# Reordering the first batch of a fused channel attention: k ahead of q, an early k norms row, zero matmuls, and folds split around the sums

## The chip, the cores and the metric

The kernel runs on one core of one Trainium2 chip. The metric is the device time of one execution in microseconds; the "span" of a profile, from the first to the last instruction, is some two microseconds shorter. Engines: PE is TensorE (matmul), PEld its weight loads, DVE is VectorE, ACT is ScalarE, POOL is GpSimd, which here starts the loads. PE is called cold while its granted clock is 0.50 (half clock). The tail is the stretch from the landing of the last piece of q and k to the first product of the main loop.

## The reference, cut to what matters

```python
def _attn_ref(q, k, v, tau):                 # q, k, v: 4 x 5824 x 256, float32
    qn = q / (np.linalg.norm(q, axis=1, keepdims=True) + 1e-06)
    kn = k / (np.linalg.norm(k, axis=1, keepdims=True) + 1e-06)
    s = kn.transpose(0, 2, 1) @ qn / tau     # 256 x 256 per batch
    a = np.exp(s - s.max(-1, keepdims=True))
    a /= a.sum(-1, keepdims=True) + 1e-09
    return v @ a
# then, on x = the result as 23296 x 256 (w1, w2: 256 x 1024; w3: 1024 x 1024; w_out: 1024 x 256):
#   ((x @ w1) * (x @ w2)) @ w3 @ w_out
```

The attention is over channels: its 256 x 256 matrix needs all 5824 rows of q and k of a batch, which are loaded in six pieces each. The kernel multiplies that matrix into w1 and w2 once per batch (the **folds**, result Wf) and w3 into w_out once (W_sb). The products of a fold land in a PSUM buffer (`psum.tile` in the code); its **drain** is the instruction on ACT or DVE that scales them and copies them to Wf. A main loop of 4 batches x 12 chunks x 8 blocks then does, per block, two products of v with Wf (a and b), the cast of a on ACT, a times b on DVE, and the product with W_sb (o).

## The kernel before: the parts concerned

The first batch has its scores made before the main loop. Squares of q and k are taken as products whose diagonal is the sum of squares.

```python
def pe_transpose(dst, src, tag, on_act):
    m = psum.tile([P, 8, P], BF16, tag=tag, ...)
    for i, blk in enumerate(src):
        nc.tensor.transpose(m[:, i, :], blk, ident_b)
    if on_act: nc.scalar.copy(dst, m)
    else:      nc.vector.tensor_copy(dst, m)
# ... first_scores(pi): for each 128-row slot of a piece, products q.k, q.q and k.k; norms_first: their diagonals
def rnorm(src):                     # 4 columns: q norms and k norms together
    r = work.tile([P, 4], F32, tag="r", ...)
    nc.scalar.activation(out=r, in_=src, func=AF.Ln)
    nc.scalar.activation(out=r, in_=r, func=AF.Exp, scale=0.5)
    nc.vector.tensor_scalar_add(r, r, 1e-6)
    nc.vector.reciprocal(r, r)
def row():                          # spreads the k norms along a row, after rnorm
    m = psum.tile([P, 512], F32, tag="ab", ...)
    for ct in range(CT):
        nc.tensor.matmul(m[:, ct * P : (ct + 1) * P],
            lhsT=st["r"][:, CT + ct : CT + ct + 1].to_broadcast([P, P]), rhs=ident, ...)
    nc.scalar.copy(kr, m[:, :C])
# ... scaled: s = G * kr (DVE), e = exp(r * s) (ACT); sums: column sums of e by 4 matmuls, reciprocal rs (DVE)
def fold(i):                        # 8 per batch
    m = psum.tile([P, 512], F32, tag="ab", ..., bufs=4)
    for c2 in range(CT):
        nc.tensor.matmul(m, lhsT=st["e"][:, c2, ...], rhs=w12[:, c2, ...], ...)
    if i % 2 == 0: nc.scalar.activation(out=dst, in_=m, func=AF.Copy, scale=st["rs"][...])
    else:          nc.vector.tensor_scalar_mul(dst, m, st["rs"][...])
# ... start of the program
for pi in range(NP_):               # 6 pieces; loads run in the order q0 k0 q1 k1 ...
    ...
    first_scores(pi)
soft0[0][1]()                                   # norms
transpose_half_on_pe(0, 0, 0, True)             # first half of v piece 0, copy on ACT
for _, fn in soft0[1:3]: fn()                   # row, scaled
transpose_half_on_pe(0, 0, 1, False)            # second half, copy on DVE
for _, fn in soft0[3:8]: fn()                   # sums, folds 0-3
```

For the later batches the same units are placed between blocks of the main loop. Each has a planned time and a planned cost; a virtual clock, advanced by these costs and by the blocks, decides behind which block a unit comes.

```python
units: norms (0.0), ss (1.0), row (0.6), scaled (0.0), sums (0.2), 8 folds (0.43 each)   # planned costs, us
ts = [t1 + 1.0, t1 + 4.0, t1 + 6.5, t1 + 8.5, t1 + 12.0] + [t1 + 13.0 + 0.9 * i for i in range(8)]
```

## Time and profile before

| | before |
|---|---|
| time, median of 3 | 585.7 us (585.57 to 585.95) |
| span | 583.6 us |
| PE busy | 564.0 us |
| first exponential (e) starts | 39.92 us |
| first a of the main loop starts | 44.35 us |

The changes of the clock are whole multiples of 3.41 us apart, so the profile was cut into stretches of that length (columns: stretch, its length, PE, PEld, DVE, ACT, POOL busy with counts, granted clock, DMA share, GB/s):

```profile
14.90:18.31 3.41, 2.63 (x36) 2.39 (x35) 0.00 (x0) 0.00 (x0) 0.78 (x3) 1.00 1.06 211
21.72:25.13 3.41, 1.45 (x20) 1.26 (x19) 0.00 (x0) 0.00 (x0) 1.06 (x2) 1.00 1.08 217
...
35.37:38.78 3.41, 1.46 (x19) 1.27 (x17) 1.73 (x4) 1.31 (x3) 1.44 (x2) 1.00 1.24 204
38.78:42.20 3.42, 2.60 (x17) 1.42 (x16) 1.68 (x5) 1.44 (x4) 0.00 (x0) 0.50 1.10 214
```

PE is busy for 1.45 of the 3.41 us before the clock falls at 25.1 us (42%). At 38.78, after a stretch with 1.46 us (43%), it falls again and stays at half over the folds. The timeline of before shows start us, duration us, engine, line, operation, out<-in, count, and in brackets the idle time of the engine and what ended it.

```profile
42.89 0.75 DVE L304 TENSOR_SCALAR Wf<-fold,rs 128x512 bf16<-128x512 f32 x1 [1.37 <-PE fold L296]
43.74 0.69 ACT L302 ACTIVATE Wf<-fold,rs 128x512 bf16<-128x512 f32 x1 [1.02 <-PE fold L296]
```

### The profile page before, as it was taken

How to read it: one execution, taken by the hardware profiler on the slowest of the kernel's cores; microseconds unless marked ns; L12 is line 12 of the kernel's file. 1: busy time of each engine (PE TensorE's matmuls, PEld its weight loads, DVE VectorE, ACT ScalarE, POOL GpSimd, SP SyncE). 2: the span in 40 equal slices, each digit the busy share in tenths (PEclk: the TensorE clock that was granted, in tenths of full speed). 3: DMA queues.
4: the chain of work that ended last, by engine and by line, in shares of the span. 5: the costliest groups of instructions: out<-in, count | busy, mean ns of one | idle time of the engine just before them, and what ended most of it. 6: DMA issues, size and time to landing. Idle time of an engine off the chain costs nothing.

```text
span 583.6 us, 10198 instructions
## 1 busy us (share of the span) xinstructions
PE 564.0 (97%) x3840; PEld 364.2 (62%) x3840; DVE 372.7 (64%) x552; ACT 339.0 (58%) x617; POOL 68.5 (12%) x145
## 2 busy tenths in 40 slices
PE   3789999999999999999999999999999999999996
PEld 3764576766666666666665766666665766566555
DVE  0026644788876567778866657777876556555564
ACT  0026635677756576767756567777766545454454
POOL 3330111221100112002100112002100000000000
PEclk9889999999999999999999999999999999999999
DMA  8999879864654699754672498764564335401011
GB/s 166 212 208 185 127 143 208 166 138 123 138 108 73 141 202 177 158 109 90 141 145 73 111 197 180 144 147 95 123 136 103 78 82 138 93 38 73 37 69 54
DMA packets 65393, 74.85 MB, mean 128 GB/s; under 512 B 45760, under 2 KB 49344, under 8 KB 65344
## 3 DMA queue, kind: packets, MB, share of 16 engines
q0 software_dynamic: 14656, 39.46, 39.1%
q1 hardware_dynamic: 50688, 34.74, 21.5%
q8 instruction: 30, 0.49, 0.3%
q14 instruction: 19, 0.16, 0.1%
HBM read 78.91 MB, written 23.86 MB: 176 GB/s over the span
## 4 chain that ended last, share of the span: by engine, by line
PE 93%; DMA 3%; DVE 1%; ACT 1%; POOL 1%; issue 1%; ACTq 0%; POOLq 0%
PE o L376 28%; PE a L354 27%; PE b L354 26%; PE G L177 5%; DMA k<-in_k_dram 3%; PE fold L296 3%; PE w L449 1%; PE G L207 1%; DVE abs L362 1%; ACT as L360 1%; PE sq L215 0%; PE sq L211 0%; PE ss L240 0%; PE row L259 0%; POOL q L106 0%
## 5 line engine op out<-in xcount | busy, mean ns | idle before, releaser
L362 DVE TENSOR_TENSOR abs<-as,b 128x512 bf16<-128x512 bf16 (+1 forms) x384 | 252.3, 658 | 158.9 <-ACT as L360 144.9
L360 ACT CAST as<-a 128x512 bf16<-128x512 f32 (+1 forms) x384 | 215.7, 562 | 174.1 <-DVE abs L362 85.3
L376 PE MATMUL o<-W_sb,abs 128*128 128x256 bf16 x1472 | 221.4, 273 | 0.2 <-DVE abs L362 0.2
L354 PE MATMUL a<-vT,Wf 128*128 128x512 bf16 x704 | 209.8, 380 | 0.1
L354 PE MATMUL b<-vT,Wf 128*128 128x512 bf16 x704 | 209.5, 379 | 0.0
L354 PEld LDWEIGHTS <-Wf 128*128 128x128 bf16 x1536 | 148.8, 98 | 97.1 <-issue 1.4
L376 PEld LDWEIGHTS <-abs 128*128 128x128 bf16 x1472 | 143.4, 98 | 86.5 <-DVE abs L362 0.4
L186 DVE TENSOR_TENSOR acc<-acc,sq 128x1024 f32<-128x1024 f32 x66 | 80.4, 1218 | 0.4 <-ACT sq L174 0.4
L346 POOL COPY gate_t<-abs 1x1 bf16<-1x1 bf16 x39 | 15.5, 398 | 396.3 <-DVE abs L362 379.6
L177 PE MATMUL G<-k,q 128*128 128x256 bf16 x276 | 50.0, 273 | 0.0
L174 ACT ACTIVATE sq<-q 128x512 f32<-128x512 bf16 x66 | 41.8, 633 | 0.0
L174 ACT ACTIVATE sq<-k 128x512 f32<-128x512 bf16 x66 | 41.6, 631 | 0.0
L207 PE MATMUL G<-k,q 128*128 128x256 bf16 x92 | 23.3, 295 | 12.0 <-DMA k<-in_k_dram 12.0
L390 DVE COPY osb<-o 128x512 f32<-128x512 f32 x44 | 30.1, 685 | 0.4 <-PE o L376 0.4
L177 PEld LDWEIGHTS <-q 128*128 128x128 bf16 x276 | 27.0, 98 | 3.1
L389 ACT COPY osb<-o 128x512 f32<-128x512 f32 x44 | 25.8, 585 | 4.0 <-PE o L376 1.9
L248 ACT ACTIVATE r<-ss 128x4 f32<-128x4 f32 x4 | 0.7, 181 | 38.5 <-DVE ss L227 35.3
L211 PE MATMUL sq<-q 128*128 128x128 bf16 x92 | 21.5, 233 | 0.0
L215 PE MATMUL sq<-k 128*128 128x128 bf16 x92 | 21.5, 233 | 0.0
L225 DVE TENSOR_TENSOR dg<-sq,ident 128x512 f32<-128x512 f32 x1 | 0.7, 691 | 31.6 <-PE sq L215 31.6
L296 PE MATMUL fold<-w,e 128*128 128x512 bf16 x64 | 17.5, 410 | 0.0
L302 ACT ACTIVATE Wf<-fold,rs 128x512 bf16<-128x512 f32 x16 | 11.0, 687 | 9.5 <-PE fold L296 9.4
(78 smaller groups left out, 199.7 us busy)
## 6 DMA issues: line engine op xcount, KB each, us to landing
out_dram<-osb SPq DMA_DIRECT2D x44, 512.0 KB, 2.8
q<-in_q_dram POOLq DMA_DIRECT2D x20, 512.0 KB, 6.1
k<-in_k_dram POOLq DMA_DIRECT2D x20, 512.0 KB, 9.0
v<-in_v_dram POOLq DMA_DIRECT2D x19, 512.0 KB, 5.2
w_bf<-in_moe_w_dram POOLq DMA_DIRECT2D x2, 1024.0 KB, 16.8
q<-in_q_dram POOLq DMA_DIRECT2D x4, 320.0 KB, 4.9
k<-in_k_dram POOLq DMA_DIRECT2D x4, 320.0 KB, 6.4
v<-in_v_dram POOLq DMA_DIRECT2D x4, 320.0 KB, 6.5
```

Of the source, the lines that this page charges most:

```text
L174: nc.scalar.activation(out=dst[:, :, part, :], in_=src[:, o : o + 2, :], func=AF.Square)
L177: nc.tensor.matmul(G[:, ct, :], lhsT=qt[:, i, ct * P : (ct + 1) * P], rhs=kt[:, i, :], start=(pr == 0 and part == 0 and ct == 0), stop=(pr ...
L186: nc.vector.tensor_add(accs[n], accs[n], sqs[0])
L207: nc.tensor.matmul(G[:, ct, :], lhsT=qt[:, i, cs], rhs=kt[:, i, :], start=(first and ct == 0), stop=(last and ct == CT - 1), skip_group_ch ...
L211: nc.tensor.matmul(S[:, ct, :], lhsT=qt[:, i, cs], rhs=qt[:, i, cs], start=(first and ct == 0), stop=False, skip_group_check=True,)
L296: nc.tensor.matmul(m, lhsT=st["e"][:, c2, c1 * P : (c1 + 1) * P], rhs=w12[:, c2, w, h * 512 : (h + 1) * 512], start=(c2 == 0), stop=(c2 == ...
L354: nc.tensor.matmul(t[:, :n], lhsT=Wf[b][:, ct, w, j * P : (j + 1) * P], rhs=rhs_of(b, c, ct), start=(ct == 0), stop=(ct == CT - 1),)
L360: nc.scalar.copy(a_sb[:, :n], tiles[0][:, :n])
L362: nc.vector.tensor_mul(ab[:, :n], a_sb[:, :n], tiles[1][:, :n])
L376: nc.tensor.matmul(tl[s // 2][:, s % 2, :], lhsT=ab[:, off : off + P], rhs=W_sb[:, j, :], start=(j == 0 and s % 2 == 0), stop=(j == FT - 1 ...
L389: nc.scalar.copy(o[:, 0:2, :], tl[0])
L390: nc.vector.tensor_copy(o[:, 2:4, :], tl[1])
```

## The change

Its intent is to have less to do after the last piece of q and k has landed. k pieces are loaded ahead of q, all held; the k norms are spread into a row by one matmul with a matrix of ones and four activations, before q is complete, so only the q norms stay in the tail. Zero matmuls keep PE's clock up. The first half of each of folds 0 and 1 runs between the two halves of the column sums. The half transpose of v, which had stood ahead of row and sums, moves behind fold 2, with its copy split between ACT and DVE; the other half moves into the main loop. The later batches use the new k row as well, with new planned costs and times. Cut below: new places for some buffers, and w1 and w2 now loaded ahead of the second half of the first v piece.

```diff
+IN_BUFS = {"q": 5, "k": 6, "v": 3}
+        if on_act is None:                                   # pe_transpose
+            nc.scalar.copy(dst[:, :4, :], m[:, :4, :])
+            nc.vector.tensor_copy(dst[:, 4:, :], m[:, 4:, :])
+    def busy(k):
+        m = psum.tile([P, 512], F32, tag="ab", ...)
+        for _ in range(k):
+            nc.tensor.matmul(m, lhsT=warm[:, :P], rhs=warm, start=True, stop=True, ...)
+        def k_row():
+            m = psum.tile([P, 512], F32, tag="ab", ...)
+            nc.tensor.matmul(m[:, :C], lhsT=ones_pp, rhs=st["ksq"], start=True, stop=True)
+            nc.scalar.activation(out=kr, in_=m[:, :C], func=AF.Ln)
+            nc.scalar.activation(out=kr, in_=kr, func=AF.Exp, scale=0.5)
+            nc.scalar.activation(out=kr, in_=kr, func=AF.Ln, bias=eps_t)
+            nc.scalar.activation(out=kr, in_=kr, func=AF.Exp, scale=-1.0)
-        head = [(0.0, norms_first)] if n == 0 else [(0.0, norms), (1.0, ss)]
-            head + [(0.6, row), (0.0, scaled), (0.2, sums)]
+        head = [(0.0, norms), (0.5, k_row), (0.4, q_sums)]
+        return head + [(0.0, scaled), (0.2, sums)] + [(0.43, lambda i=i: fold(i)) for i in range(8)]
+        def first_folds():
+            sum_mm(0)
+            fold_mm(0, 0)
+            fold_mm(1, 0)
+            sum_mm(1)
+            fold_mm(0, 1)
+            fold_mm(1, 1)
+            fold(2)
+            transpose_half_on_pe(0, 0, 0, None)
+            fold(3)
 # ... start of the program, from the first q piece; cut: the loads and squares of k0 and k1, with 22 zero matmuls
+    for pi in range(3):
+        products(pi, whole)
+        squares("q", pi, whole)
+        squares("k", pi + 2, whole)
+        busy(4)
 # ... cut: loads of q4 k5 q5, w1/w2, v
+    products(3, whole); squares("q", 3, whole)
+    products(4, whole); squares("q", 4, whole)
+    squares("k", 5, range(LAST + 1), end=True)
+    soft0[0](); busy(2); soft0[1]()              # diagonal of k, k row
+    squares("q", 5, first)
+    products(5, first)
+    squares("q", 5, rest, end=True)
+    soft0[2]()                                   # diagonal and norms of q
+    products(5, rest, end=True)
+    soft0[3]()                                   # s, e
+    busy(6)
+    soft0[4]()                                   # first_folds
 # ... in the main loop
+            at(4.0, 0.5, lambda: transpose_half_on_pe(0, 0, 1, False))
-        ts = [t1 + 1.0, t1 + 4.0, t1 + 6.5, t1 + 8.5, t1 + 12.0] + [t1 + 13.0 + 0.9 * i for i in range(8)]
+        ts = [t1 + 1.0, t1 + 3.5, t1 + 4.0, t1 + 8.0, t1 + 12.0] + [t1 + 13.0 + 0.9 * i for i in range(8)]
```

## The prediction

> **What bounds the kernel now.** I read the engine summary first, then the slices, then what TensorE (PE) waited for.
>
> ```profile
> PE 564.0 (97%) x3840; PEld 364.2 (62%) x3840; DVE 372.7 (64%) x552; ACT 339.0 (58%) x617; POOL 68.5 (12%) x145
> ...
> PE   3789999999999999999999999999999999999996
> ...
> PEclk9889999999999999999999999999999999999999
> DMA  8999879864654699754672498764564335401011
> ```
>
> PE is busy 564.0 of 583.6 us, so at most 19.6 us of idle can be removed; whatever it does cold (half clock) comes on top. The slices (14.6 us each) put the loss into the first three, before the main loop, and a little into the last. The waits of PE over the whole run say the same:
>
> ```profile
> PE G L207 <- DMA k<-in_k_dram: 12.0, 3, 8.9
> PE row L259 <- DVE r L251: 1.9, 1, 1.9
> PE sum L281 <- ACT e L274: 0.8, 2, 0.6
> ```
>
> Three waits for k pieces are 12.0 us, then 2.7 us in the softmax. No wait of size lies in the later batches. But the DMA itself is full in this stretch, as the five-microsecond windows show (columns: PE, PEld, DVE, ACT, POOL, granted clock, DMA share, GB/s):
>
> ```profile
> 10.00:15.00 5.00, 4.95 (x58) 4.47 (x57) 0.00 (x0) 0.00 (x0) 0.96 (x2) 1.00 1.08 216
> 15.00:20.00 5.00, 3.85 (x53) 3.53 (x51) 0.00 (x0) 0.00 (x0) 2.37 (x7) 1.00 1.05 211
> 25.00:30.00 5.00, 5.00 (x49) 4.42 (x47) 0.00 (x0) 0.00 (x0) 1.36 (x3) 0.66 1.08 206
> 40.00:45.00 5.00, 4.30 (x14) 1.68 (x15) 2.29 (x6) 2.20 (x4) 0.00 (x0) 0.50 1.09 210
> ```
>
> So the 12.0 us are the arrival of data at about 212 GB/s (bytes written) and mostly stay. What can go is the lag behind the last arrival. First q and k pieces are usable at 6.45 and 8.85 us, then a 512 KB piece every 2.47 us; ten pieces and two of 352 KB (1.7 us each) end at about 32.6, while the last product starts at 35.48. From there the timeline shows a serial tail:
>
> ```profile
> 35.90 0.69 DVE L225 TENSOR_TENSOR dg<-sq,ident 128x512 f32<-128x512 f32 x1 [31.55 <-PE sq L215]
> ...
> 38.02 0.18 DVE L251 RECIPROCAL r<-r 128x4 f32<-128x4 f32 x1
> 38.26 0.76 PE L259 MATMUL row<-ident,r 128*128 128x128 f32 x4 [1.95 <-DVE r L251]
> ...
> 39.92 0.91 ACT L274 ACTIVATE e<-s,r 128x256 bf16<-128x256 f32 x2 [0.49 <-DVE s L271]
> ...
> 40.99 3.57 PE L296 MATMUL fold<-w,e 128*128 128x512 bf16 x8
> ...
> 44.35 1.06 PE L354 MATMUL a<-vT,Wf 128*128 128x512 bf16 x2
> ```
>
> The folds run cold: eight 512-column matmuls are issued over 3.4 us, 0.43 us each; two lines later in the same trace warm ones are 0.21 us apart. The main loop starts at **44.35**; from there PE hardly stops.
>
> **What the Trainium skill says.** "TensorE: Matmul & The Clock Gate", Part 1, says the PE clock is halved by an activity monitor with a free-running window of about 3.4 us, and that sustained activity restores it. The trace agrees: one-microsecond windows put the changes near 11.5, 25.1, 28.5, 38.8 and 45.6 us, gaps that are multiples of 3.41 us. The page asks for about an idle window; here the window 21.7 to 25.1 had a 1.96 us wait, about 42% busy, and was followed by half clock, while 14.9 to 18.3, about 78% busy, was not. I estimate the limit lies between. Part 4 of the page adds that transposes don't count as PE activity; the trace doesn't separate that. "DMA: Bandwidth & Descriptors", Bandwidth, has 425 GB/s measured for a 16 MB load by one core whose neighbour idles; the loads here read twice what they write (f32 to bf16), some 424 GB/s, which agrees, so I take 2.47 us a piece as the floor.
>
> **The change part by part.**
>
> 1. *k ahead of q.* Same bytes, same queue, one order: k0, k1, q0, k2, q1, k3, q2, k4, q3, q4, k5, q5. By the cadence above q4 is there at 29.2, k5 at 30.9, q5 at 32.6. Gain by itself: none; it frees the k norms from the tail.
>
> 2. *Zero matmuls.* 42 of 512 columns, 0.21 us each warm. Those of the piece loop (4 per pair, 0.85 us) join 2.64 us for a q piece (16 products at 0.11, 16 squares at 0.055) and 0.88 for k: 4.4 of the 4.94 us that a pair takes to arrive, so they hide and keep the clock up. Before, half clock from 25.1 to 28.5 cost 1.7 us.
>
> 3. *The last pieces.* PE: q3 from 26.7 to 29.35, q4 to 32.0, k5 squares to 32.65, the diagonal on DVE (256 columns, 0.42, the duration of s) beside two zero matmuls to 33.1, k row matmul to 33.7, five q squares and products to 35.35, last two squares 35.46. So PE still ends its q work near 35.5, now warm with k done, as products of two q pieces are bunched at the end. The four activations of the k row, about 0.45 us each (copy of kr 0.37, e 0.50), end near 35.6, beside the q work.
>
> 4. *The tail.* Diagonal of q 35.55 to 35.95, its sum (half of 0.69) to 36.33, two activations (0.21 each) to 36.8, two small DVE operations to 37.22, s to 37.67, the first e to 38.2, the second to 38.65. Before, e ended at 40.83: 2.2 us earlier. Gone are the row matmul and its copy (1.2 us); dg and ss are halved (0.7).
>
> 5. *Folds split around the sums.* First half-folds go beside the second e. Reciprocals end at 39.3; ACT drains folds 0 and 2 (0.69 each) to 40.7 and half a transpose copy (0.55) to 41.25; DVE fold 1, the other half copy and fold 3 (0.75, 0.35, 0.75) to 41.15. Main loop start: **41.3, 3.05 us earlier**. First a and b matmuls, then warm, take 0.85 instead of 1.49 us: 0.6 more. The second half transpose moves into the PE-bound loop: 8 at 0.055, minus 0.45.
>
> 6. *Later batches.* PE work in the loop, before: eight passes of ss between 434.37 and 435.19, four of row between 436.48 and 436.93, 1.27 us a batch. After: half the ss passes (0.41) and two 256-column passes, estimated at 0.43 from 0.11 for 128 columns: 0.84. Three batches save 1.3 us. Against it ACT gets four 256-column activations in a row where one copy was, 1.4 us more; at 58% busy and four PSUM buffers I expect at most a few tenths lost on PE.
>
> Sum: 3.05 + 0.6 - 0.45 + 1.3 - 0.3 (ACT) = **4.2 us**, so 581.5.
>
> **The rivals.** *Clock falls again:* between the six zero matmuls (end 36.75) and the first sum (38.24) PE idles 1.5 us. If one activity window takes all of it, it is 56% busy, inside my uncertain band; folds and first a and b would be cold, costing 1 to 1.7 us: about 583. I give this three in ten. For it: the same happened at 38.8 before; against it: that window was mostly idle. *Weights as the new wait:* w1 and w2 now precede all but half of v0; first halves land at 32.6 plus 2.47, 35.1, well before 38.2, and the second near 38.8, used after 41. w3's halves landed about 47.9 and 52.9 (their time to landing) and its transposes began at 57.2: more than 4 us to spare. I expect no new wait. *Everything hidden anyway:* if arrival alone set the end, time would be unchanged, 585.5; against it, 11.7 us lie between the last arrival and the main loop, none of them DMA. *Better than thought:* if kr and G wait for less and the drains overlap, 579.5.
>
> **Range and chances.** Expected **581.5 us**. The phase of the activity window gives +1.7 at worst, the loop term -1.3 to +1, the tail about 1 either way: **579.7 to 583.4** for 8 in 10. Two per cent is 11.7 us, over half the PE idle of the whole run, most of which is arrival: faster by over 2% has 0.02, slower 0.01, within 2% 0.97.
>
> **What would show it right or wrong.** The last q piece should land near 32.6 and PE end its q products near 35.5; PE's clock should be 1.00 from about 12 us through the folds; e should end near 38.6; the first a matmul should start near 41.3; w3 transposes should have no DMA wait. The PE time of ss and row per batch should fall from 1.27 to about 0.84 us. The prediction is wrong if the clock at the folds reads 0.5, if the main loop starts later than 43, if the load order opens a hole in the DMA row, or if ACT's burst makes PE wait in each later batch.

## The result, and the profile after

The changed kernel took **583.33 us** (583.27 to 583.53, 4 runs) beside 585.63 us (584.72 to 585.95, 4 runs) of the kernel before: ratio 0.9964, 95% interval 0.9946 to 0.9981, the same within 2%. A ratio here is the record's, over the fast runs of both kernels, and not quite the ratio of the medians. The result is inside the predicted range, but the gain is 2.1 us by spans (583.63 to 581.53) and 2.3 by medians, about half of the 4.2 us that the steps summed to.

What the kernel before loses to half clock differs between its own executions. In the rounds of the experiments it ran 23 times: seven times at a mean clock of 0.997, in 584.8 us on average, and sixteen times at 0.989 to 0.993, in 585.6. The profiled one (0.989) is of the second kind, so part of the gain by spans depends on which execution was profiled.

The summary and slices of the changed kernel's page:

```profile
PE 569.3 (98%) x3862; PEld 363.1 (62%) x3862; DVE 374.2 (64%) x565; ACT 342.7 (59%) x629; POOL 64.4 (11%) x139
...
PE   7989999999999999999999999999999999999996
...
PEclk9999999999999999999999999999999999999999
```

PE is busy 5.3 us longer than before though the span is shorter, as the 42 zero matmuls alone keep it busy for 12.1 us: busy time says nothing of progress. The first three slices read 7, 9, 8 instead of 3, 7, 8. What PE waited for (us in total, times, longest):

```profile
PE sqk L226 <- DMA k<-in_k_dram: 2.2, 2, 1.9
PE warm_I-91_92 L214 <- DVE warm L78: 1.3, 1, 1.3
PE G L238 <- DMA q<-in_q_dram: 1.2, 3, 0.5
PE sum L310 <- ACT e L301: 1.2, 1, 1.2
PE a L402 <- DVE vT L137: 1.0, 1, 1.0
```

Of the 12.0 us of waits for k, 8.9 of them for the first piece, 2.2 are left, and 1.2 for q: the rest is filled with squares and zero matmuls. The wait of the row matmul for the reciprocal (1.9 us) is gone. In its place stands one that before did not have: the first a waits 1.0 us for a copy of transposed v by DVE. Two of the five-microsecond windows that the prediction showed of before, now of after:

```profile
25.00:30.00 5.00, 4.69 (x54) 3.74 (x52) 0.00 (x0) 0.00 (x0) 1.44 (x3) 1.00 1.08 206
...
40.00:45.00 5.00, 4.02 (x26) 1.86 (x25) 2.57 (x5) 3.40 (x6) 0.00 (x0) 1.00 1.08 209
```

The clock, 0.66 and 0.50 in these windows before, is 1.00 in both. The timeline of after, from the k row to the first a:

```profile
33.56 0.70 PE L268 MATMUL row<-dk,ones_pp 128*128 128x256 f32 x2
...
36.06 0.42 DVE L254 TENSOR_TENSOR dq<-sqq,ident 128x256 f32<-128x256 f32 x1 [2.55 <-PE sqq L226]
...
38.17 0.91 ACT L301 ACTIVATE e<-s,r 128x256 bf16<-128x256 f32 x2 [0.76 <-DVE s L298]
...
39.91 1.26 ACT L336 ACTIVATE Wf<-fold,rs 128x512 bf16<-128x512 f32 x2 [0.83 <-PE fold L329]
...
41.06 0.58 ACT L136 COPY vT<-tr_I-527_528 128x512 bf16<-128x512 bf16 x1
41.68 0.42 DVE L137 COPY vT<-tr_I-527_528 128x512 bf16<-128x512 bf16 x1 [1.01 <-ACT vT L136]
...
42.16 0.59 PE L402 MATMUL a<-vT,Wf 128*128 128x512 bf16 x2 [0.98 <-DVE vT L137]
```

The first e starts at 38.17 instead of 39.92, 1.75 us earlier. From there to the first a it takes 3.99 us, where before took 4.43 **at half clock**. DVE stood idle for 1.01 us before its half of the copy and was released by the ACT half. Taking the start of every block's a in both traces, the lead of after over before goes like this:

| at | lead, us |
|---|---|
| first e | 1.75 |
| first a | 2.19 |
| after the first blocks (a, b at full clock) | 2.80 |
| after the half transpose in the loop | 2.35 |
| end of batch 0's own work | 2.20 |
| after the transitions into batches 1, 2, 3 | 2.20, 2.16, 2.12 |

So nothing of the forecast saving in the later batches arrived. To see why, the time from each PE instruction's start to the next one's was summed by group over 24 blocks around the transition into batch 2 (into batch 3 it is the same):

The times are in us:

| kernel | total | o | a | b | fold | ss | row | sum |
|---|---|---|---|---|---|---|---|---|
| before | 30.433 | 9.17 | 8.23 | 8.22 | 3.45 | 0.81 | 0.45 | 0.10 |
| after | 30.468 | 9.17 | 8.26 | 8.22 | 3.92 | 0.36 | 0.43 | 0.10 |

The norms take 0.47 us less (1.26 to 0.79). The folds take 0.47 us more.

### The profile page after: what moved, and what is told of

The parts are those of the page before. It is cut to its first block, busy times and chain, and to the rows that moved or that the text cites. A ratio compares the mean times of both kernels' runs of the same rounds, so it can differ in the third digit from the quotient of the medians.

```text
span 581.5 us, 10244 instructions
## 1 busy us (share of the span) xinstructions
PE 569.3 (98%) x3862; PEld 363.1 (62%) x3862; DVE 374.2 (64%) x565; ACT 342.7 (59%) x629; POOL 64.4 (11%) x139
## 4 chain that ended last, share of the span: by engine, by line
PE 90%; DMA 3%; DVE 2%; ACT 1%; issue 1%; POOL 1%; ACTq 0%; POOLq 0%
PE o L424 27%; PE a L402 26%; PE b L402 26%; PE G L193 5%; DMA q<-in_q_dram 3%; PE fold L329 2%; PE w L530 1%; DVE abs L410 1%; ACT as L408 1%; PE G L238 1%; POOL k L119 1%; PE sqq L226 0%; PE row L268 0%; DVE osb L438 0%; POOL q L119 0%
## 5 line engine op out<-in xcount | busy, mean ns | idle before, releaser
L394 POOL COPY gate_t<-abs 1x1 bf16<-1x1 bf16 x39 | 12.4, 318 | 393.2 <-DVE abs L410 376.8
L193 PE MATMUL G<-k,q 128*128 128x256 bf16 x276 | 50.2, 273 | 0.0
L270 ACT ACTIVATE kr<-row 128x256 f32<-128x256 f32 x4 | 1.5, 383 | 34.9 <-PE row L268 34.9
L119 POOL DMA_DIRECT2D q<-in_q_dram x25 | 13.5, 540 | 11.1 <-DMA k<-in_k_dram 5.0
L119 POOL DMA_DIRECT2D v<-in_v_dram x24 | 12.9, 537 | 11.7 <-DMA vT<-v 4.6
L119 POOL DMA_DIRECT2D k<-in_k_dram x25 | 13.8, 552 | 2.8 <-DMA k<-in_k_dram 2.0
L338 DVE TENSOR_SCALAR Wf<-fold,rs 128x512 bf16<-128x512 f32 x16 | 11.7, 747 | 1.6 <-PE fold L329 1.5
```

The lines of the kernel that those rows point to most:

```text
L119: nc.gpsimd.dma_start(out=t[:, lo:hi, :], in_=main[:, pi * PIECE + lo : pi * PIECE + hi, :])
L193: nc.tensor.matmul(G[:, ct, :], lhsT=qt[:, i, ct * P : (ct + 1) * P], rhs=kt[:, i, :], start=(pr == 0 and part == 0 and ct == 0), stop=(pr ...
L394: nc.gpsimd.tensor_copy(gate_t, last_ab[0][:1, :1])
```

## The experiments

Two questions were put. Where do the two halves of the missing gain go (the tail ahead of the main loop; the later batches)? And which part of the change makes what gain there is? All kernels gave correct results. Each was timed in rounds with the kernel before (585.1 to 585.7 us median in those rounds).

| run | edit | median us (range) | ratio to before |
|---|---|---|---|
| e1 | two banks for the half transpose | 583.10 (582.91–583.35) | 0.9955 |
| e7 | half transpose ahead of the sums | 582.19 (581.93–582.41) | 0.9944 |
| e4 | folds not split | 583.69 (583.58–583.80) | 0.9964 |
| e6 | q norms and row in another order | 582.21 (582.14–583.25) | 0.9949 |
| e5 | later folds planned 0.8 later | 582.37 (582.35–582.93) | 0.9951 |
| e2 | planned costs raised | 583.53 (583.35–583.67) | 0.9962 |
| e3 | no zero matmuls | 583.46 (583.31–584.67) | 0.9965 |
| e11 | before, with zero matmuls | 583.43 (583.36–583.51) | 0.9971 |
| e8 | e5, e6 and e7 together | 580.09 (579.75–580.47) | 0.9909 |
| e9 | e8, k row planned later | 581.43 (581.35–581.61) | 0.9937 |
| e10 | e8 without zero matmuls | 580.19 (580.17–581.07) | 0.9919 |

These are read against the changed kernel's 583.33 us by medians, and by the stages of the trace where half a microsecond matters: profiled executions of one and the same early code differ by up to 0.53 us at the first e (38.07 in e7, 38.60 in e2), with the time at which pieces land (q3 landed at 26.87 us in the changed kernel, 27.30 in e2).

### The tail: the half transpose

**e1: two tiles, so two PSUM banks, for the two half copies.** "PSUM — Partial Sum Buffer" of the Trainium skill, section "PSUM bank collisions raise a hardware error", says that two engines must not be on one bank and quadrant at once, ScalarE against VectorE reads included, and that they have to be put in turn by semaphores. The copies in the change share one tile of one bank.

```diff
+        if on_act is None:
+            for h in range(2):
+                m = psum.tile([P, 4, P], BF16, tag=tag, ...)
+                # ... 4 transposes each; copy of half 0 on ACT, of half 1 on DVE
```

> Edit: the first half transpose of v, which the changed kernel copies out of one PSUM tile with half on ScalarE and half on VectorE, is written to two PSUM tiles of four blocks, one for each engine. Theory A (the two copies take turns only because they read one PSUM bank): the VectorE copy starts right after fold 1's drain, near 40.7 us instead of 41.68, fold 3's drain ends near 41.85 instead of 42.76, and the first a matmul starts near 41.7 instead of 42.16, so the whole run gains 0.4 to 0.6 us. Theory B (they take turns because they write one SBUF tile, or VectorE was busy anyway): the VectorE copy still starts after the ScalarE copy ends, near 41.65, and nothing changes within 0.1 us.

Timeline of e1:

```profile
40.92 0.42 DVE L140 COPY vT<-tr_I-534_535 128x512 bf16<-128x512 bf16 x1
41.20 0.59 ACT L138 COPY vT<-tr_I-527_528 128x512 bf16<-128x512 bf16 x1
```

DVE now copies ahead of ACT and overlaps with it. The first a is at 41.83; from the first e (38.30) that is 3.53 us, 0.46 less than in the changed kernel. Theory A holds against B: the copies still write one SBUF tile, so the turn-taking came with the shared PSUM tile, and it cost 0.46 us. The page's reason, the bank, fits, but e1 gave each copy its own tile together with its own bank, so it doesn't tell the two apart. By medians the run gained 0.23, less than the 0.4 to 0.6 expected.

**e7: the half transpose ahead of the sums again**, copy on DVE alone, where PE and DVE wait for the exponentials anyway.

```diff
-            transpose_half_on_pe(0, 0, 0, None)      # in first_folds
     busy(6)
+    transpose_half_on_pe(0, 0, 0, False)
     soft0[4]()
```

> Edit: the first half transpose of v goes ahead of the sums, where PE idles, and its whole copy goes to VectorE; folds 2 and 3 follow each other. Theory A (the two half copies, one behind the other and behind the drains, start the main loop late): the copy runs behind s, at about 38.5 to 39.2 us, the first a matmul starts at 40.7 to 40.9 instead of 42.16 and the first b near 41.2, the run gains 1.0 to 1.3 us. Theory B (drains of the folds set the start by themselves): the first a matmul starts at 41.9 or later, the run gains under 0.3 us. Risk in both: if the half piece of v lands after 38.5, PE waits for it ahead of the sums.

Timeline of e7:

```profile
38.28 0.68 DVE L141 COPY vT<-tr_I-506_507 128x1024 bf16<-128x1024 bf16 x1
...
40.55 0.61 PE L401 MATMUL a<-vT,Wf 128*128 128x512 bf16 x2
```

The copy of the whole tile lies inside the two exponentials (38.07 to 38.98). From first e to first a it is 2.48 us, 1.51 less than in the changed kernel. By medians the run gains 1.14. Theory A holds: the place of the transpose is the largest single loss of the change.

**e4: sums whole, then folds 0 and 1 whole**, to price the split.

```diff
-            sum_mm(0); fold_mm(0, 0); fold_mm(1, 0); sum_mm(1); fold_mm(0, 1); fold_mm(1, 1)
+            sums(); fold(0); fold(1)
```

> Edit: the first folds are not split; all four column sums come first, then folds 0, 1, 2, the half transpose and fold 3. Theory A (drains wait for the reciprocals, which need the second e in either order; the split hides only matmul time): fold 0's drain starts within 0.1 us of 39.91, the first a matmul starts 0 to 0.3 us later than 42.16. Theory B (the split brings the drains forward): fold 0's drain and the first a matmul both start 0.4 us or more later.

First e to first a became 4.19 us instead of 3.99, and the median rose by 0.36. The split is worth 0.2 us in the chain: the sums, and with them the drains' scale, come slightly earlier without it, but the folds later. Theory A holds.

### The tail: the q norms

**e6: squares of q first, then the k row, then the last products; half of s made ahead of the q norms' small DVE operations.**

```diff
     soft0[0]()
-    busy(2)
-    soft0[1]()
     squares("q", 5, first)
-    products(5, first)
     squares("q", 5, rest, end=True)
     soft0[2]()
+    soft0[1]()
+    products(5, first)
     products(5, rest, end=True)
 # and: s of column half 0 (DVE), then q_norm, then s of half 1, then e
```

> Edit: in the first batch, all squares of the last q piece come straight behind those of the last k piece, then the k row, then the last products; the two zero matmuls ahead of the k row are out; the first product with the k row goes ahead of the reciprocal norms of q on VectorE. Theory A (PE runs late behind the last load, and the k row, its wait and the zero matmuls stand on the way to the end): the q squares end 2 us earlier, the first e starts at 37.0 to 37.3 us instead of 38.17, the first a matmul at 41.0 to 41.3, the run gains 0.9 to 1.2 us. Theory B (the last loads or the ScalarE chain of the k row set the end): the first e starts within 0.3 us of 38.17 and nothing is gained.

The profiled execution was the slowest of the four: its k5 landed at 32.66 us instead of 31.07. Still its first e started at 38.13; from the last q piece's landing to e it took 3.9 us, against 5.2 in the changed kernel. The other three ran at 582.14 to 582.27, 1.1 faster than the changed kernel. By its first e alone this execution would meet theory B; the other three, and e8 below, decide for A (in e8, q5 landed at 33.13 and the first e started at 37.03, 3.9 us later again). Theory A holds: the order of the work behind the last landings held the chain of the q norms back by about 1.1 us. The edit changes three things at once, the order on PE, two zero matmuls fewer ahead of the k row and the earlier half of s; no run tells their shares apart.

### The later batches

**e5: folds planned 0.8 us later**, so that a block lies between the sums and fold 0, as it did before.

```diff
-        ts = [...] + [t1 + 13.0 + 0.9 * i for i in range(8)]
+        ts = [...] + [t1 + 13.8 + 0.9 * i for i in range(8)]
```

> Edit: in the later batches the folds are planned 0.8 later behind the sums and nothing else is moved, so that in batches 2 and 3 one block of a, b and o stands between the sums and fold 0, while the norms and the exponentials keep the places of the changed kernel. Theory A (fold 0 directly behind the sums costs 0.47 us in each of these two batches): the time of the folds in each of the two transitions falls from 3.92 to about 3.45 us, a, b and o stay as they are, the run gains 0.8 to 1.0 us. Theory B (ScalarE is overloaded around the softmax and the wait only changes its place, as when the planned costs were raised: folds minus 0.47, o plus 0.31, a plus 0.06 us): the folds gain 0.47 us but a, b and o lose most of it, the run gains under 0.3 us.

The timeline around the sums for batch 2. In the kernel before, a block lies between sums and folds, and six fold matmuls run together in 1.46 us:

```profile
442.13 0.24 PE L281 MATMUL sum<-ones_b,e 128*128 128x1 bf16 x4
442.23 0.59 PE L354 MATMUL a<-vT,Wf 128*128 128x512 bf16 x2
...
443.53 1.46 PE L296 MATMUL fold<-w,e 128*128 128x512 bf16 x6
```

In the changed kernel fold 0 directly follows the sums, and the six after the block take 1.63:

```profile
440.84 0.24 PE L310 MATMUL sum<-ones_b,e 128*128 128x1 bf16 x4
...
440.95 0.59 PE L329 MATMUL fold<-w,e 128*128 128x512 bf16 x2
...
442.50 0.69 ACT L336 ACTIVATE Wf<-fold,rs 128x512 bf16<-128x512 f32 x1 [1.09 <-PE b L402]
442.67 1.63 PE L329 MATMUL fold<-w,e 128*128 128x512 bf16 x6
443.08 0.58 ACT L408 CAST as<-a 128x512 bf16<-128x512 f32 x1
```

Fold 0 was ready from 441.5, but ACT drained it only at 442.50. The bracket names PE's b as what ended ACT's idle time; the drain also needs the reciprocal of the sums, which DVE finished at 442.41, behind a copy of outputs, and that is the later one. One of the four PSUM buffers was held meanwhile, and the cast of the block's a, which frees another, was pushed behind that drain to 443.08. In e5:

```profile
440.41 0.24 PE L310 MATMUL sum<-ones_b,e 128*128 128x1 bf16 x4
...
440.51 0.59 PE L402 MATMUL a<-vT,Wf 128*128 128x512 bf16 x2
...
441.81 1.03 PE L329 MATMUL fold<-w,e 128*128 128x512 bf16 x3
```

The transitions into batches 2 and 3 take 30.01 us instead of 30.47, with the folds at 3.45 again and a, b, o unchanged. The run is 0.96 us faster. Theory A holds: the saved 0.47 us per batch had been given back by fold 0 behind the sums.

**e2: the planned costs of k_row and q_sums raised** from 0.5 and 0.4 to 0.9 and 0.7, to move the virtual clock instead of the plan.

```diff
-        head = [(0.0, norms), (0.5, k_row), (0.4, q_sums)]
+        head = [(0.0, norms), (0.9, k_row), (0.7, q_sums)]
```

> Edit: only the planned costs of the two new softmax units of later batches are raised from 0.5 and 0.4 to 0.9 and 0.7, whose sum is that of the units that they replaced; no instruction changes, only where folds land among the main loop's matmuls. By the instruction order, folds of batches 2 and 3 then stand as in the kernel before (one block of a, b and o between the sums and fold 0) and those of batch 1 stand directly behind the sums. Theory A (the 0.47 us that each later batch saves on the norms is given back because fold 0 stands directly behind the sums and holds a PSUM buffer and ScalarE until the reciprocals come): the transition into batch 2 and into batch 3 gets 0.45 us shorter each, the one into batch 1 gets 0.3 to 0.5 us longer. Theory B (ScalarE's four activations in a row cause it): folds wait 0.47 us in batches 2 and 3 as before, no transition changes by more than 0.1 us.

For batches 2 and 3 the folds fell from 3.92 to 3.45 us as expected, but o rose from 9.17 to 9.48 and a from 8.26 to 8.32: 0.10 net each. The raised costs also brought the exponentials one block closer to the four activations of the k row, and a casts queued behind both. Into batch 1 it lost 0.17. Each theory was right in part: the fold's place is the cause, but four activations of 256 columns stayed free in these runs only with room around them.

**e9: on e8 below, k row and q sums planned 1.7 us later**, so that PE would not wait for the sum of squares in batch 1. There before took 30.869 and after 30.868 us in total: the norms' saving was given back ahead of the row matmul, which now comes one block earlier than ss had and waits for DVE's sum of squares; the time is booked to the o before it, 9.49 instead of 9.17, and to row, 0.54 instead of 0.45.

```diff
-        ts = [t1 + 1.0, t1 + 3.5, t1 + 4.0, ...
+        ts = [t1 + 1.0, t1 + 5.2, t1 + 5.7, ...
```

> Edit: the three edits together, and in the later batches the k row and the q sums are planned 1.7 later, one block of a, b and o further behind the sum of the squares. Theory A (in the transition into batch 1 PE waits about 0.43 us for that sum): o falls from 9.49 to 9.17 and row from 0.54 to 0.43 us there, the run gains 0.3 to 0.45 us against the three edits together. Theory B (the room between the k row and the exponentials, now one block less, is too small and ScalarE's burst meets the exponentials): that transition gains but others lose as much; no gain.

It lost 1.3 us against e8. Into batch 1 the row fell to 0.43 us, but o rose to 10.06 and the total to 31.527; into batches 2 and 3 it was 30.365 instead of 30.006. PE's a waited 0.71 us for an ACT cast: the four activations now met the exponentials, and the cast stood behind these. ACT itself was idle for 1.09 us just ahead of the exponentials, waiting for s from DVE, which points to the order on ACT beside its load. Theory B holds. The wait of batch 1 is real and could not be taken back by this move.

### The zero matmuls

**e3: the changed kernel without zero matmuls.**

```diff
     def busy(k):
+        return
```

> Edit: the zero matmuls are left out, all else as in the changed kernel. Theory A (they keep the clock up, and that is worth its cost): the granted clock falls to 0.5 in some stretch before the main loop, above all at the folds, and the first a matmul starts 1 us or more later than 42.16; run longer by 1 to 3 us. Theory B (the new order of loads and squares spreads the work enough): clock stays at 1.00 through 36 us and at most the folds are cold, run longer by under 1 us, or even shorter, as two zero matmuls stand ahead of the k row on the way to the end.

Three of four executions ran at 583.31 to 583.47, like the changed kernel; one took 584.67 at a mean clock of 0.994. In the profiled one the clock was 1.00 from 13.7 us on, and first e to first a was 3.99 us, the same. Its least busy stretch of 3.41 us:

```profile
20.51:23.92 3.41, 1.68 (x16) 1.52 (x17) 0.00 (x0) 0.00 (x0) 0.53 (x1) 1.00 1.05 210
```

49% busy was enough here, where 42% was not before. In the new order PE keeps itself busy enough in most executions; the zero matmuls insure against the rest (Theory B).

**e10: e8 without zero matmuls.**

> Edit: the three edits together, without any zero matmul. Theory A (the zero matmuls are an insurance: whether a gap halves the clock depends on where the 3.41 us windows fall in that execution): most executions within 0.2 us of those with zero matmuls, mean clock 0.998 or above, and one in three to five of them 0.8 to 2 us longer with a mean clock of 0.997 or below. Theory B (they do nothing at all in this order): all executions as fast, clock 0.998 or above in all. Theory C (they are needed): all 1 us or more longer.

The median is 580.19, as e8's, but one of five executions took 581.07 at a clock of 0.995. With e3, two of nine executions without zero matmuls were about 1 us longer; of the 40 with them none had a clock under 0.998. The two longer ones were not profiled, so where their clock fell was not seen. Insurance again (Theory A of this run).

**e11: the kernel before, with zero matmuls and nothing else**: four after each of the first four pairs, eight after the first half transpose, six after the second.

```diff
         first_scores(pi)
+        if pi < 4:
+            busy(4)
     transpose_half_on_pe(0, 0, 0, True)
+    busy(8)
 ...
     transpose_half_on_pe(0, 0, 1, False)
+    busy(6)
```

> Edit: to the kernel before only zero matmuls are added, four behind each of the first four pairs of pieces, eight behind the first half transpose and six behind the second. Theory A (half clock is most of what the kernel before loses ahead of the main loop): the granted clock stays at 1.00 from about 12 us on, the eight fold matmuls are issued in 1.7 to 1.9 us instead of 3.4, the first a matmul starts at 42.0 to 42.8 instead of 44.35, the run gains 2.0 to 3.0 us, as much as the whole change. Theory B (the drains, the softmax chain and the arrivals set it, clock matters little): the first a matmul starts later than 43.5 and the run gains under 1 us.

Timeline of e11:

```profile
39.83 0.91 ACT L282 ACTIVATE e<-s,r 128x256 bf16<-128x256 f32 x2 [0.49 <-DVE s L279]
...
40.88 1.89 PE L304 MATMUL fold<-w,e 128*128 128x512 bf16 x8
...
42.60 0.59 PE L362 MATMUL a<-vT,Wf 128*128 128x512 bf16 x2
```

The first e is where it was (39.83 against 39.92): the half clock from 25.1 to 28.5 us cost 0.1 us, or 0.3 counted from the last k piece's landing (32.65 before, 32.85 in e11), as the data set the pace there. The folds, now at full clock, take 1.89 us for eight where before took 3.57, and first e to first a 2.77 instead of 4.43. The lead by the first blocks is 2.01 us and stays. At 583.43 us, this is within 0.1 us of the whole change. Beside the kernel before in the same rounds the gains are 1.6 us for e11 and 2.3 for the change; the ratios, 0.9971 (0.9957 to 0.9984) and 0.9964 (0.9946 to 0.9981), have overlapping intervals.

### Together

**e8: e5, e6 and e7 on the changed kernel.** Its diff is the sum of theirs.

> Edit: the three edits together. If each of the three theories A holds and they add up: first e near 37.1, first a matmul near 39.7, each of the two later transitions 0.45 us shorter, the run 2.7 to 3.5 us shorter than the changed kernel, near 580.1. If the half piece of v (landed at 36.8) or the weights (first halves landed at 35.5, second at 39.3) become the wait, the first a matmul starts after 40.3 and the gain is under 2.5.

580.09 us (579.75 to 580.47, 4 runs), ratio to before 0.9909 (0.9894 to 0.9924): 3.24 us below the changed kernel, as the parts summed to, and ahead of both kernels. Timeline of e8:

```profile
37.03 0.91 ACT L266 ACTIVATE e<-s,r 128x256 bf16<-128x256 f32 x2 [0.57 <-DVE r L300]
...
39.51 0.60 PE L411 MATMUL a<-vT,Wf 128*128 128x512 bf16 x2
```

First e is at 37.03, and first e to first a takes 2.48 us. The transitions take 30.871, 30.006 and 30.006 us. One thing is left in the tail: the sums for the q norms were ready at 34.64, but their activations started at 36.03, behind the four of the k row on ACT. No run tried the other order.

## Why the prediction was right and wrong

The total lay inside the range and the class was right; the sum was twice the gain. By its steps:

1. *k ahead of q, no gain by itself* — right. The last of q5 landed at 32.99 us in the changed kernel (32.6 foreseen), and the last k piece at 32.65 before.
2. *Zero matmuls* — the clock was 1.00 from 5 us on to the main loop, as foreseen, and "before, half clock from 25.1 to 28.5 cost 1.7 us" was wrong: e11 shows it cost 0.1 to 0.3, hidden behind the arrival. It was not in the sum, so it cost nothing there. The rival "clock falls again", given three in ten, did not come about in any profiled execution.
3. *The last pieces* and 4. *The tail*, "the first e to 38.2, the second to 38.65" — off by 0.43 us: the second e ended at 39.08. The k row started at 33.56, not at 33.1, the diagonal of q at 36.06, not 35.55; q3 had landed about 0.2 late, and the diagonals start some 0.2 after the last square is issued. e6 shows that 1.1 us of this chain is a matter of order.
5. *Folds split around the sums*, "Main loop start: 41.3" — it was 42.16. Besides the 0.43 just told, the failed term is "half a transpose copy (0.55) to 41.25; DVE fold 1, the other half copy": the two copies were put side by side, but they share one PSUM tile, so one bank, and took turns (e1: 0.46). I had not asked what it costs to move the transpose behind the folds at all (e7: 1.51 in the chain). The first a and b at full clock gained 0.61 (0.6 foreseen), and the half transpose in the loop cost 0.45 as foreseen.
6. *Later batches*, "Three batches save 1.3 us ... I expect at most a few tenths lost on PE" — **the step that failed most.** The PE time of ss and row did fall as worked out, from 1.26 to 0.79 us (0.84 foreseen), but all of it was given back: in batches 2 and 3 by fold 0 directly behind the sums (e5: 0.46 each), in batch 1 by PE waiting for the k row's sum of squares. The diff showed the lower planned costs and earlier times; I counted the work of the units and not where they now fall among the blocks.

The shortfalls are 0.43 (e), 0.43 (copies), about 1.1 (later batches) and 0.15 (rest of batch 0), together 2.1 of the 4.2 us. The 0.15 was seen only as waits shifted from b to a among the w3 transposes; no run tested it, so its cause stays open.

The attribution was off as well. The change brings the softmax 1.75 us forward and lifts the clock over the folds, worth 1.66 us of the chain in e11 (4.43 to 2.77). With both in place and the first half transpose ahead of the sums (e7), 2.48 us lie between e and a. The change itself has 3.99: most of what the warm clock gives, its own new order behind the exponentials takes back. This is how a large rearrangement comes to be worth about as much as fourteen idle-time matmuls near the folds and sixteen in the piece loop.

## What to carry to other kernels

When a change shortens one chain, ask what it moved into the next: here work that had lain in waiting time (a transpose and its copy) was moved behind the last wait, where every tenth counts, and took back most of the gain. When planned costs or times of interleaved work change, look at where each unit now falls and which buffer it holds, not only at its own duration. Before a rearrangement, try the smallest part alone: here keeping the clock up was worth about as much as the whole.

## What the Trainium skill lacked or had wrong

- "TensorE: Matmul & The Clock Gate", Part 1: asks for about an idle window before the clock halves. Here two windows of 3.41 us with PE busy for 42% (1.45 us, longest wait 1.96 us) and 43% (1.46 us) were followed by half clock; one at 48% (1.63 us, 7.83 to 11.25 in the changed kernel) and one at 49% (e3) were not; the limit between is not given. It says that one busy window restores the clock, but not how busy: 100% did (42.2 to 45.6 us before), and so did 77% (2.63 us, 8.06 to 11.48; matmuls were issued at 10 a us before that and 17 after), but 76% at 38.8 to 42.2 did not. Of this last window 1.06 us were transposes, of the other none, which fits the passage on transposes that the prediction cites from Part 4; one window of each kind does not prove it.
- The same page says that the window's phase varies from run to run. What that may cost a kernel with gaps, here: without zero matmuls 2 of 9 executions were 0.9 and 1.2 us longer, at mean clocks of 0.995 and 0.994. That the phase made the difference is not shown, as neither was profiled.
- "PSUM — Partial Sum Buffer", bank collisions: right, but it gives no cost for the turn-taking that follows. Splitting a copy of one tile in one bank between ACT and DVE (0.58 and 0.42 us) left DVE idle for 1.01 us; a tile and bank for each saved 0.46 us (e1).
- No page that I used prices a chain of activations inside a matmul-bound loop: four of 256 columns (0.38 to 0.51 us each) left the whole saving of PE in batches 2 and 3 where they stood well ahead of the exponentials (e5), and cost 0.36 to 0.66 us a batch where they met them (e9).
